# Moving a head's scores within SBUF: one DMA of 120 rows instead of two of 60

## The chip, the cores and the metric

The program runs on one core of a Trainium2 chip. The metric is the device time of one execution in microseconds. The kernel before takes 1316.79 us in the median of three runs (1316.54 to 1318.35).

## The reference

Talking-heads attention, then two feed-forward stages, all in float32 (batch 4, 12 heads, 448 positions, head size 64):

```python
scores = scale * np.matmul(q, k.transpose(0, 1, 3, 2))
scores = np.einsum('bhij,hg->bgij', scores, w_pre)        # mixes the heads
scores = scores - np.max(scores, axis=-1, keepdims=True)
attn = np.exp(scores)
attn = attn / (np.sum(attn, axis=-1, keepdims=True) + 1e-09)
attn = np.einsum('bhij,hg->bgij', attn, w_post)           # mixes the heads again
x = np.matmul(attn, v)                                    # rows of 12 * 64 = 768
h = ((x @ w1) * (x @ w2)) @ w3 @ w_out
h = h @ w_in2
out = np.maximum(0.01 * h, h) @ w_out2
```

## The kernel before

Attention comes first, the feed-forward stages (called MoE in the code) follow. Everything in attention is issued in an order written out by hand (`manual_schedule`, line 114): on each engine and each DMA queue the instructions stand in program order. The feed-forward part is ordered by a planner, with a few edges to attention's instructions (`issue_after`).

**Tiles.** The 448 query positions of a batch are cut into chunks of 120, 120, 120 and 90 (`CH` is 120; the last chunk is padded from 88 to 90). There are 16 chunks. The heads go in six pairs. `qk(b, c, p)` (line 178) multiplies a pair: two products of 120 x 448 scores into PSUM, one for each head. `out` (line 191) evicts them to a tile `s` (two heads, six buffers); ScalarE does both, except in the first eight calls (`early`), where VectorE takes the second head.

**The move.** Mixing the heads needs the heads along the partitions. So each head's scores are moved within SBUF by DMA from `s`, where a partition is a query position, to a tile `sr`, where 12 partitions of each of 10 groups are the heads of one query position (`move`, line 207). A DMA carries 60 rows of 448 floats, six to each of 10 destination partitions. A chunk of 120 has two such halves in two `sr` tiles; five tiles are used in turn (`SUB = 6`, lines 126 and 183). The last head needs two DMAs for a half, since its partitions wrap. So a chunk costs 26 DMAs, all issued by SyncE's queue (SP). The host has laid out the query columns (`_deal`, line 936) so that rows land in the right places.

**The mix and what follows.** `premix(k)` (line 240) is the first mix, for a group of 20 query positions: it reads two rows of the tile `sr`. A chunk has six groups, the last chunk of a batch five; there are 92 groups. The loop at line 406 handles two groups in one pass, `k` and `k + 1`. In the order of the code a pass does: stores of finished outputs (`flush`); `qk` for the pairs that groups `k + 8` and `k + 9` bring (`LEAD` is 8); row maxima on VectorE (`tops`); exponentials on ScalarE (`softmax`); the evictions and moves of this pass's pairs (`evict`); products with the values (`av`, line 314); division by the sums (`weigh`); the second mix of the pass before and its transposes (`postmix`); loads of later queries, keys and values (`side`); the first mix of groups `k + 2` and `k + 3`.

A chunk's first group needs all six pairs. The groups of a batch are 23, an odd count. In batches 0 and 2 a chunk starts on an even group, and its last pair is evicted one pass before its first `premix`. In batches 1 and 3 a chunk starts on an odd group, and its last pair is evicted and moved in the very pass whose end holds its first `premix`. The exception is the last chunk of a batch, whose last two pairs come a pass earlier.

**The start.** Before the loop the first eight groups' pairs (chunk 0 and two pairs of chunk 1) are multiplied, evicted and moved, and `premix(0)` and `premix(1)` follow. The `sr` tiles are zeroed first (`constants_load`, line 132).

**The end of attention.** The feed-forward part loads the attention output of two batches into `x` (line 648) behind entries of the list `reads`, which holds the moves in the order of issue: `XREADS = (-5, -3)`. The splitting of `x` on ScalarE and VectorE (`halves`) is placed behind the ends of certain passes (`XMARKS`). After the loop, lines 440 to 448 finish the remaining `av` products.

Of the kernel before, what the change touches and what calls it, by code (L numbers as in the profile page):

```python
# [8 lines left out]
F32 = mybir.dt.float32  # L9
# [13 lines left out]
def attention_moe_kernel(ctx: ExitStack, tc, qt, kt, vt, w_pre, w_post, w1, w2, w3t, w_out, w_in2, w_out2, out):  # L23
# [7 lines left out]
    nc = tc.nc  # L31
    B, _, NPAIR, S = kt.shape
# [6 lines left out]
    P = 128  # L39
    JP = 112  # L40
    NJ = S // JP
    IB = 10
    LEAD, SUB, GAP = 8, 6, 13
    CH = qt.shape[-1]
    scale = 1.0 / float(D) ** 0.5

# [3 lines left out]
    i0 = 0  # L50
# [17 lines left out]
    def bank(shape, name):  # L68
        return ps.tile(shape, F32, tag="bank", name=name, bufs=8)
# [34 lines left out]
    ends, reads, marks = {}, [], []  # L104

    def attention():
        with ExitStack() as es:
            ld = es.enter_context(tc.tile_pool(name="a_ld", bufs=2))
            big = es.enter_context(tc.tile_pool(name="a_big", bufs=1))
            const = es.enter_context(tc.tile_pool(name="a_const", bufs=1))  # L110
# [5 lines left out]
            HR, Q = HQ * H, P // 2  # L116
# [5 lines left out]
            kpre = const.tile([P, Q], F32, name="kpre")  # L122
            kpost = const.tile([P, 2, 32], F32, name="kpost")
            mask = const.tile([P, 2, HQ], F32, name="mask")
            eye = const.tile([P, HQ * GAP], F32, name="eye")
            rows_of = [const.tile([P, SUB, S], F32, name=f"sr{i}") for i in range(5)]
            wrep = const.tile([P, 2, H], F32, name="wrep")

            ones = const.tile([P, P], F32, name="ones")
# [1 line left out]

            def constants_load():
                for i, t in enumerate(rows_of):
                    (nc.gpsimd if i > 1 else nc.vector).memset(t, 0.0)
                for t in (kpre, kpost, eye):
                    nc.gpsimd.memset(t, 0.0)
                for n, w in enumerate((w_pre, w_post)):
                    nc.sync.dma_start(out=wrep[:, n, :], in_=w)
# [22 lines left out]
            vst, srt = {}, {}  # L161
            pms, mxs, ets, apt = {}, {}, {}, {}
# [15 lines left out]
            def qk(b, c, p, early=False):  # L178

                m = cols[c]  # L180
                if p == 0:
                    for i, n0 in enumerate(range(0, m, SUB * IB)):
                        srt[b, c, i] = rows_of[len(srt) % len(rows_of)], n0, min(SUB, (m - n0) // IB)
                t = big.tile([CH, 2, S], F32, tag="s", name="s", bufs=6)
                pq = [bank([CH, S], "pq") for _ in range(2)]
                for e in range(2):
                    rows = slice(e * D, (e + 1) * D)
                    nc.tensor.matmul(  # L188
                        pq[e][:m], qls[b, c][rows, p, :m], kls[b, p // 2][rows, p % 2, :], start=True, stop=True
                    )  # L190
                def out():
                    for e in range(2):
                        if e and early:
                            nc.vector.tensor_copy(t[:m, e, :], pq[e][:m])
                        else:
                            nc.scalar.activation(out=t[:m, e, :], in_=pq[e][:m], func=ACTF.Copy)  # L196
                    for e in range(2):
                        h = 2 * p + e
                        for i in range(2):
                            if (b, c, i) in srt:  # L200
                                move(srt[b, c, i], t[:, e, :], h)

                evs.append(out)
                if early:
                    evict()

            def move(sr, t, h):

                dst, n0, w = sr
                if h < H - 1:  # L210
                    parts = [(h, 0, 2 * HQ)]
                else:
                    parts = [(h, 0, HQ), (Q, HQ, HQ)]
                for r0, i0, n in parts:
                    reads.append(nc.sync.dma_start(  # L215
                        out=dst[r0:r0 + GAP * (n - 1) + 1:GAP, :w, :],
                        in_=t[n0 + i0 * w:n0 + (i0 + n) * w, :],
                    ))
                ends["sync"] = reads[-1]

            evs = []

# [17 lines left out]
            def premix(k):  # L240

                b, c, t, _ = where[k]
                i, u = divmod(t, SUB // 2)
                sr = srt[b, c, i][0]
                ns = groups[k]
                for n in ns:
                    pms[n] = bank([P, S], "pm")
                for s in range(2):
                    rows = slice(s * Q, (s + 1) * Q)
                    for g in range(len(ns)):  # L250
                        half = (g if len(ns) > 1 else s) * Q
                        nc.tensor.matmul(  # L252
                            pms[ns[s % len(ns)]][half:half + Q], kpre[rows], sr[rows, 2 * u + g, :],
                            start=True, stop=True,
                        )

# [17 lines left out]
            def weigh(ns, sm, e, last):  # L274

                m = len(ns)
                nc.vector.tensor_scalar(out=sm[:, :m], in0=sm[:, :m], scalar1=1e-9, scalar2=None, op0=ALU.add)
                rc = wk.tile([P, 2 * HB], F32, tag="rc", name="rc", bufs=2)
                ends["dve"] = nc.vector.reciprocal(out=rc[:, :m], in_=sm[:, :m])  # L279
                shares = (nc.gpsimd, nc.scalar, nc.vector, nc.scalar) if last else (nc.gpsimd,) * 3 + (nc.vector,)  # L280
                for i, eng in enumerate(shares[:m]):
                    if eng is nc.scalar:
                        ends["act"] = eng.activation(out=e[:, i], in_=e[:, i], func=ACTF.Copy, scale=rc[:, i:i + 1])
                        continue
                    ends["dve" if eng is nc.vector else "pool"] = eng.tensor_scalar(  # L285
                        out=e[:, i], in0=e[:, i], scalar1=rc[:, i:i + 1], scalar2=None, op0=ALU.mult
                    )
# [61 lines left out]
            for b, c in order:  # L349
                ns = [n for n, x in enumerate(blocks) if x[:2] == (b, c)]  # L350
# [54 lines left out]
            todo = []  # L405
            for k in range(0, NG + 2, 2):
                if k:
                    flush()
                while later:
                    stores.append(later.pop(0))  # L410
                now = [g for g in (k, k + 1) if g < NG]
                done = [g for g in (k - 2, k - 1) if g >= 0]
                fresh = [n for g in now for n in groups[g]]
                old = [n for g in done for n in groups[g]]
                before = ets.pop(k - 2, None)
                ahead = [x for g in now if g + LEAD < NG for x in slot(g + LEAD)]
                for x in ahead:
                    qk(*x)
                if fresh:
                    tops(fresh)  # L420
                    sm, ets[k] = softmax(fresh)
                evict()
                if now:
                    for _ in range(min(4 if len(todo) > NPAIR else 2, len(todo))):
                        av(*todo.pop(0))
                    weigh(fresh, sm, ets[k], not ahead)
                while lows:
                    lows.pop(0)()
                if old:
                    postmix(old, before)  # L430
                side(k // 2)
                for g in done:
                    b, c, t, nt = where[g]
                    if t == nt - 1 and (b, c) != order[-1]:
                        todo += [(b, c, p) for p in range(NPAIR)]
                for g in (k + 2, k + 3):
                    if g < NG:
                        premix(g)
                marks.append(dict(ends))
            while todo:  # L440
                av(*todo.pop(0))
            flush()
            for p in range(NPAIR):
                av(*order[-1], p)
# [491 lines left out]
def _deal(q, width=120):  # L936

    import numpy as _np

    n, h, s, d = q.shape  # L940
    places = []
    for c0 in range(0, s, width):
        at = [c0] * width
        for o in range(0, min(width, s - c0 + 2), 60):
            w = min(6, (s - c0 + 2 - o) // 10)
            for i in range(10):
                for m in range(w):
                    half, k = divmod(i, 5)
                    if m == w - 1 and w % 2:
                        to = 20 * (m // 2) + 5 * half + k  # L950
                    else:
                        to = 20 * (m // 2) + 10 * half + 5 * (m % 2) + k
                    at[o + i * w + m] = min(c0 + o + to, s - 1)
        places.append(at)
    places = _np.array(places)
    t = q[:, :, places, :].reshape(n, h // 2, 2, *places.shape, d)
    return t.transpose(0, 3, 2, 5, 1, 4).reshape(n, len(places), 2 * d, h // 2, width)
# [39 lines left out]
```

## Time and profile before

| | |
|---|---|
| median of 3 runs | 1316.79 us |
| the profiled execution | 1318.09 us |
| its span | 1316.3 us |
| TensorE matmul busy | 1240.1 us (94%) |
| VectorE busy | 892.1 us (68%) |
| ScalarE busy | 523.1 us (40%) |
| mean granted TensorE clock | 0.966 |
| DMAs of `sr<-s` | 416, of which 308 of 105 KB, 100 of 52.5 KB, 8 of 26.2 KB |

The span is what the profiler recorded from the first to the last instruction; the execution is 1.8 us longer. Engine names in rows: PE is TensorE's matmul, DVE VectorE, ACT ScalarE, POOL GpSimd, SPq SyncE's queue. In the rows `sr<-s` is the move, L252 the first mix, L188 `qk`, L329 `av`, L305 the second mix, L196 and L194 the evictions. The granted clock is a share of full speed: 1.00 is 2.4 GHz, 0.50 is 1.2 GHz.

### The profile page before, as it was taken

To read this page: it belongs to the slowest core of one execution; us is meant where nothing else is said; L and a number is where in the kernel's file an instruction comes from. 1 tells how busy PE (TensorE), PEld (TensorE's weight loads), DVE (VectorE), ACT (ScalarE), POOL (GpSimd) and SP (SyncE) were. 2 spreads that over 40 slices of the span, in tenths; PEclk is the share of its full clock that TensorE was granted. 3 is DMA by queue.
4 is the path that set the end of the run, shared out by engine and by line. 5 is a ranking of instruction groups with operands and counts; after the bars stand their busy time and mean duration, and the time that the engine had idled before them with its cause. 6 is when DMAs were issued, how large, how long until landed. Compare 5 with 4: busy or idle time off the path is not lost.

```text
span 1316.3 us, 22208 instructions
## 1 busy us (share of the span) xinstructions
PE 1240.1 (94%) x8616; PEld 981.9 (75%) x8616; DVE 892.1 (68%) x1552; ACT 523.1 (40%) x1024; POOL 195.6 (15%) x142
## 2 busy tenths in 40 slices
PE   5888989987897899999999999999999999999998
PEld 3233434443343589999889999999999999999998
DVE  3665657666566899983579596856877657394763
ACT  2645455544444455542235452335232333431220
POOL 2544445445442000000000000000000000000000
PEclk7888889999898899999999999999999999999999
DMA  4554544654533577563985463605342212212112
GB/s 153 171 158 139 167 136 127 176 161 139 167 110 127 185 243 235 178 205 136 357 308 191 169 208 127 218 25 204 107 126 84 80 55 73 72 43 67 30 49 84
DMA packets 124969, 190.51 MB, mean 145 GB/s; under 512 B 21600, under 2 KB 104640, under 8 KB 124480
## 3 DMA queue, kind: packets, MB, share of 16 engines
q1 hardware_dynamic: 124864, 189.10, 45.0%
q8 instruction: 68, 1.11, 0.4%
q14 instruction: 37, 0.30, 0.1%
HBM read 111.03 MB, written 39.32 MB: 114 GB/s over the span
## 4 chain that ended last, share of the span: by engine, by line
PE 80%; DMA 6%; DVE 5%; ACT 4%; SPq 3%; issue 1%; POOLq 0%; ACTq 0%; DVEq 0%
PE pm L480 27%; PE po L495 18%; PE pp L770 16%; PE pw L561 5%; DMA sr<-s 5%; PE pq L188 5%; PE pm L252 4%; SPq L215 3%; PE px L329 3%; DVE ap L312 3%; PE po L305 3%; ACT e L269 2%; ACT s L196 2%; DMA scr<-y 1%; DVE mx L262 1%
## 5 line engine op out<-in xcount | busy, mean ns | idle before, releaser
L480 PE MATMUL pm<-x,ws 128*128 128x384 f32 (+1 forms) x1152 | 233.9, 364 | 0.6 <-DVE ws L75 0.6
L480 PEld LDWEIGHTS pm<-x,ws 128*128 128x128 f32 x1152 | 208.7, 188 | 24.8 <-DVE ws L75 1.0
L285 POOL TENSOR_SCALAR e<-e,rc 128x448 f32<-128x448 f32 x130 | 187.9, 1458 | 244.0 <-DVE rc L279 204.2
L269 ACT ACTIVATE e<-pm,mx 128x448 f32<-128x448 f32 x180 | 111.9, 632 | 201.9 <-DVE mx L262 201.7
L252 PE MATMUL pm<-sr,kpre 64*64 64x448 f32 x720 | 104.2, 619 | 56.8 <-DMA sr<-s 52.6
L262 DVE TENSOR_REDUCE mx<-pm 128x1 f32<-128x448 f32 x180 | 100.3, 606 | 52.5 <-PE pm L252 52.3
L252 PEld LDWEIGHTS pm<-sr,kpre 64*64 64x64 f32 x720 | 30.9, 144 | 126.3 <-issue 87.1
L770 PE MATMUL pp<-t,w 128*128 128x448 f32 x576 | 124.5, 368 | 0.0
L312 DVE STREAM_TRANSPOSE ap<-po 128x512 f32<-128x512 f32 (+3 forms) x216 | 115.1, 592 | 13.1 <-PE po L305 12.0
L495 PE MATMUL po<-ws,g 128*128 128x384 f32 x672 | 117.2, 334 | 0.0
L495 PE MATMUL po<-wo,g 128*128 128x384 f32 x672 | 117.1, 334 | 0.0
L495 PEld LDWEIGHTS po<-wo,g 128*128 128x128 f32 x672 | 116.6, 188 | 0.2
L495 PEld LDWEIGHTS po<-ws,g 128*128 128x128 f32 x672 | 116.6, 188 | 0.0
L770 PEld LDWEIGHTS pp<-t,w 128*128 128x128 f32 x576 | 108.1, 188 | 10.9
L329 PEld LDWEIGHTS px<-ap,vs 96*64 96x64 f32 (+1 forms) x1536 | 80.4, 140 | 36.0 <-ACT e L269 21.0
L305 PE MATMUL po<-e,kpost 64*32 64x512 f32 (+1 forms) x1472 | 92.9, 598 | 11.9 <-ACT e L269 6.2
L188 PE MATMUL pq<-kl,ql 64*120 64x448 f32 (+1 forms) x384 | 97.5, 619 | 0.0
L770 PE MATMUL pp<-b,w 128*128 128x448 f32 x432 | 95.6, 368 | 0.0
L196 ACT ACTIVATE s<-pq 120x448 f32<-120x448 f32 (+1 forms) x184 | 86.0, 559 | 15.8 <-PE pq L188 13.4
L329 PE MATMUL px<-ap,vs 96*64 96x120 f32 (+3 forms) x1536 | 90.1, 271 | 2.0 <-DVE ap L312 1.2
L502 DVE TENSOR_TENSOR acc<-po,acc 128x384 f32<-128x384 f32 x84 | 45.3, 553 | 68.3 <-PE po L495 68.2
L91 ACT ACTIVATE wc<-wr 128x768 f32<-128x768 f32 (+1 forms) x72 | 61.6, 858 | 72.3 <-DMA wr<-in_moe_w_dram 21.6
(102 smaller groups left out, 1521.3 us busy)
## 6 DMA issues: line engine op xcount, KB each, us to landing
sr<-s SPq DMA_DIRECT2D x308, 105.0 KB
wr<-in_moe_w_out_dram SPq DMA_DIRECT2D x24, 768.0 KB
wr<-in_moe_w_dram SPq DMA_DIRECT2D x16, 768.0 KB
wr<-in_moe_w_in_dram SPq DMA_DIRECT2D x16, 768.0 KB
wr<-in_moe_w_dram SPq DMA_DIRECT2D x16, 512.0 KB
kept_w<-wc SPq DMA_DIRECT2D x16, 384.0 KB
sa<-kept_w SPq DMA_DIRECT2D x16, 384.0 KB
sums_w<-su SPq DMA_DIRECT2D x8, 768.0 KB
```

The costliest lines, as they stand in the source:

```text
L188: nc.tensor.matmul(pq[e][:m], qls[b, c][rows, p, :m], kls[b, p // 2][rows, p % 2, :], start=True, stop=True)
L196: nc.scalar.activation(out=t[:m, e, :], in_=pq[e][:m], func=ACTF.Copy)
L252: nc.tensor.matmul(pms[ns[s % len(ns)]][half:half + Q], kpre[rows], sr[rows, 2 * u + g, :], start=True, stop=True,)
L262: nc.vector.tensor_reduce(out=mxs[n], in_=pms[n], axis=AX.X, op=ALU.max, negate=True)
L269: ends["act"] = nc.scalar.activation(out=e[:, i], in_=pms.pop(n), func=ACTF.Exp, bias=mxs.pop(n), scale=1.0, accum_out=sm[:, i:i + 1])
L285: ends["dve" if eng is nc.vector else "pool"] = eng.tensor_scalar(out=e[:, i], in0=e[:, i], scalar1=rc[:, i:i + 1], scalar2=None, op0=ALU.mult
L305: nc.tensor.matmul(po[g][32 * r:32 * (r + 1), :m], kpost[rows, x], e[rows, :m, JS[r]:JS[r] + P], start=True, stop=True,)
L312: ends["dve"] = nc.vector.transpose(out=dst, in_=po[g][:, i0:i1])
L329: nc.tensor.matmul(px[e * D:(e + 1) * D, r, :nw].rearrange("p (n i) -> p n i", i=HQ), vst[b][rows, jc, 2 * p + e, :], ap[rows, x, :ns, jc, ...
L480: nc.tensor.matmul(dst, wt[:, a, kk, :], x[kk][:, c, c0:c0 + w], start=(kk == order[0] and j == 0), stop=(kk == order[-1] and j == 2),)
L495: nc.tensor.matmul(po, g[m][:, a, t * P:(t + 1) * P], wts[m][:, c, cs], start=(m == 0 and j == 0), stop=(m == FQ - 1 and j == 2),)
L770: nc.tensor.matmul(dst, w[:, i, a, kk, :], b[:, kk, c, :], start=(kk == 0 and j == 0), stop=(kk == KH - 1 and j == 2),)
```

## The change

A head's scores of a whole chunk go in one DMA: 120 rows, 12 to each of 10 destination partitions; the last head in two DMAs of 60 rows. A chunk has one `sr` tile of 12 rows, and three such tiles are used in turn. The tile `s` has five buffers instead of six. In the first eight calls (`early`) ScalarE's queue issues the move of the first head of a pair; everything else stays on SP. The remaining `av` products of the pass that has no new groups are placed ahead of its second mix instead of after the loop. `_deal` lays out the queries for whole chunks. `XREADS` is not edited; the list it counts in has half as many entries.

```diff
-    LEAD, SUB, GAP = 8, 6, 13
+    LEAD, GAP = 8, 13
...
-            rows_of = [const.tile([P, SUB, S], F32, name=f"sr{i}") for i in range(5)]
+            rows_of = [const.tile([P, CH // IB, S], F32, name=f"sr{i}") for i in range(3)]
...
-                    (nc.gpsimd if i > 1 else nc.vector).memset(t, 0.0)
+                    (nc.gpsimd if i else nc.vector).memset(t, 0.0)
...
                 if p == 0:
-                    for i, n0 in enumerate(range(0, m, SUB * IB)):
-                        srt[b, c, i] = rows_of[len(srt) % len(rows_of)], n0, min(SUB, (m - n0) // IB)
-                t = big.tile([CH, 2, S], F32, tag="s", name="s", bufs=6)
+                    srt[b, c] = rows_of[len(srt) % len(rows_of)]
+                t = big.tile([CH, 2, S], F32, tag="s", name="s", bufs=5)
...
                     for e in range(2):
-                        h = 2 * p + e
-                        for i in range(2):
-                            if (b, c, i) in srt:
-                                move(srt[b, c, i], t[:, e, :], h)
+                        move(srt[b, c], t[:m, e, :], 2 * p + e, nc.sync if e or not early else nc.scalar)
...
-            def move(sr, t, h):
-
-                dst, n0, w = sr
+            def move(dst, t, h, queue):
+
+                m = t.shape[0]
+                w = m // IB
...
                 for r0, i0, n in parts:
-                    reads.append(nc.sync.dma_start(
-                        out=dst[r0:r0 + GAP * (n - 1) + 1:GAP, :w, :],
-                        in_=t[n0 + i0 * w:n0 + (i0 + n) * w, :],
-                    ))
-                ends["sync"] = reads[-1]
+                    ends["sync"] = queue.dma_start(
+                        out=dst[r0:r0 + GAP * (n - 1) + 1:GAP, :w, :], in_=t[i0 * w:(i0 + n) * w, :]
+                    )
+                    reads.append(ends["sync"])
...
-                i, u = divmod(t, SUB // 2)
-                sr = srt[b, c, i][0]
+                sr = srt[b, c]
...
-                            pms[ns[s % len(ns)]][half:half + Q], kpre[rows], sr[rows, 2 * u + g, :],
+                            pms[ns[s % len(ns)]][half:half + Q], kpre[rows], sr[rows, 2 * t + g, :],
...
                     weigh(fresh, sm, ets[k], not ahead)
+                else:
+                    while todo:
+                        av(*todo.pop(0))
                 while lows:
                     lows.pop(0)()
...
-            while todo:
-                av(*todo.pop(0))
             flush()
```

## Rows read from the trace of the kernel before

**Rows 1.** Busy time of each engine in stretches; then granted clock, DMA share, GB/s.
```profile
14.00:26.00 12.00, 0.14 (x2) 0.00 (x0) 1.53 (x5) 0.54 (x1) 0.00 (x0) 0.69 0.43 130
52.00:60.00 8.00, 8.00 (x66) 2.63 (x62) 5.34 (x10) 4.65 (x12) 3.02 (x3) 0.75 0.94 239
100.00:150.00 50.00, 42.63 (x506) 19.74 (x502) 31.55 (x72) 24.29 (x67) 24.67 (x18) 0.90 0.56 160
125.00:131.00 6.00, 6.00 (x23) 2.14 (x21) 1.59 (x4) 2.90 (x8) 1.79 (x2) 0.50 0.54 140
500.00:550.00 50.00, 50.00 (x250) 44.95 (x249) 48.30 (x75) 24.78 (x37) 0.00 (x0) 1.00 0.63 202
```

**Rows 2.** Who waited for whom in attention: us in total, times, longest.
```profile
PE pm L252 <- DMA sr<-s: 52.6, 12, 14.4
```

**Rows 3.** Timeline of SP's queue: start, duration, operation, count.
```profile
7.52 28.24 SPq L215 DMA_DIRECT2D sr<-s  x34
...
396.69 11.30 SPq L215 DMA_DIRECT2D sr<-s  x14
```

**Rows 4.** Source line 215: ns min/median/max of one issue, first and last start.
```profile
L215 SPq DMA_DIRECT2D sr<-s x416: 712/748/2812, 7.5 to 407.3; - x139
```

**Rows 5.** Timeline at the start of attention, ScalarE and TensorE.
```profile
9.66 0.54 ACT L196 ACTIVATE s<-pq 120x448 f32<-120x448 f32 x1 [2.16 <-PE pq L188]
...
28.52 3.78 PE L252 MATMUL pm<-sr,kpre 64*64 64x448 f32 x16 [14.38 <-DMA sr<-s]
```

**Rows 6.** The chain that ended last, in pieces: start, duration, what.
```profile
42.15 2.54 DMA sr<-s
...
48.39 2.29 DMA sr<-s
...
131.13 7.59 DMA sr<-s
...
146.05 1.73 ACT s L196 x4
...
407.26 1.99 DMA sr<-s
```

**Rows 7.** Timeline of TensorE, first mixes of chunks in batches 0 and 2.
```profile
50.78 4.12 PE L252 MATMUL pm<-sr,kpre 64*64 64x448 f32 x16 [3.96 <-DMA sr<-s]
...
77.47 4.03 PE L252 MATMUL pm<-sr,kpre 64*64 64x448 f32 x16 [4.22 <-DMA sr<-s]
...
229.19 2.11 PE L252 MATMUL pm<-sr,kpre 64*64 64x448 f32 x16 [1.59 <-DMA sr<-s]
...
281.70 3.42 PE L252 MATMUL pm<-sr,kpre 64*64 64x448 f32 x16 [4.04 <-DMA sr<-s]
...
307.32 2.07 PE L252 MATMUL pm<-sr,kpre 64*64 64x448 f32 x16 [1.12 <-DMA sr<-s]
```

**Rows 8.** Timeline of TensorE around first mixes of chunks in batches 1 and 3.
```profile
141.11 1.74 PE L252 MATMUL pm<-sr,kpre 64*64 64x448 f32 x16
142.78 1.77 PE L188 MATMUL pq<-kl,ql 64*120 64x448 f32 x8
...
147.80 0.98 PE L252 MATMUL pm<-sr,kpre 64*64 64x448 f32 x8
151.59 2.48 PE L252 MATMUL pm<-sr,kpre 64*64 64x448 f32 x8 [2.81 <-DMA sr<-s]
154.01 3.35 PE L188 MATMUL pq<-kl,ql 64*120 64x448 f32 x8
...
382.51 2.14 PE L252 MATMUL pm<-sr,kpre 64*64 64x448 f32 x8 [1.65 <-issue]
```

**Rows 9.** End of attention: TensorE's timeline, and a piece of the chain.
```profile
407.45 1.68 PE L252 MATMUL pm<-sr,kpre 64*64 64x448 f32 x8 [1.31 <-DMA sr<-s]
...
409.38 6.35 DMA x<-scr
...
440.27 2.82 PE L305 MATMUL po<-e,kpost 64*32 64x384 f32 x32 [4.23 <-POOL e L285]
```

More of the change, by code (lines that the diff above doesn't have):

```diff
@@ L943, in _deal @@
         at = [c0] * width
[L944 to L953, printed above, removed]
+        w = min(width, s - c0 + 2) // 10
+        for i in range(10):
+            for m in range(w):
+                half, k = divmod(i, 5)
+                to = 5 * half if m == w - 1 and w % 2 else 10 * half + 5 * (m % 2)
+                at[i * w + m] = min(c0 + 20 * (m // 2) + to + k, s - 1)
         places.append(at)
```

## The prediction

> **What bounds the kernel now.** I read first the busy time by stretches. TensorE is busy for all of a stretch of the feed-forward part, at the full clock; in attention it is busy 42.6 us of 50, at a mean clock of 0.90 [rows 1]. So the second part has nothing to give, and it starts when attention's last results are there: a microsecond saved in attention is a microsecond of the whole. The list of waits says what TensorE lacks in attention: its first mix waited 52.6 us for moves, in 12 places, the longest 14.4 us [rows 2]. Then SP's timeline: the first 34 moves occupy the queue without a break for 28.24 us, that is 0.83 us each, and the last 14 for 11.30 us, 0.81 us each [rows 3]. An issue takes 712 ns at least and 748 ns in the median over moves of 15 to 60 rows [rows 4]; its cost goes by the count of DMAs, not by their rows. A pass with two new pairs issues 8 to 10 of them, 6.5 to 8.3 us, and a pass of TensorE at full clock, from one `premix` to the next, takes 147.80 - 141.11 = 6.7 us [rows 8]. SP is the engine that can't keep up. Last I read TensorE's own timeline where a chunk begins: it stops there [rows 7, 8], and what runs after a long stop runs slowly. The stretch from 125 to 131 us, behind such a stop, shows the granted clock at 0.50, the 1.2 GHz level [rows 1].
>
> **Part 1: the start.** `premix(0)` begins at 28.52 us after 14.38 us of idling [rows 5]. It waits for the 23rd issue of SP, at 0.83 us each, and its landing. After the change it needs 13 moves, 7 on SP and 6 on ScalarE. ScalarE's cycle for a pair is one eviction (0.54 us [rows 5]) and one issue (0.8 us, taken as on SP [rows 4]), some 1.4 us, so five pairs after 9.66 us end by 16.9 us; SP is done earlier. Then the transfers limit. The highest rate in my rows is 239 GB/s, at a DMA share of 0.94 [rows 1]; a move of 215 KB needs 0.90 us at it. The first move of the second pair goes out at about 9.66 + 0.54 + 0.05 = 10.25 us. It lands 3.2 us later (below), nine more heads follow at 0.90 us: 10.25 + 3.2 + 8.1 = 21.5 us. The gain is 28.5 - 21.5 = **7.0 us**. Bounds: 9.5 us if issue alone limits (last issue 16.1 us, landing 19); nothing or a loss of 2 us if ScalarE's issues cost twice as much and its evictions wait behind them. The five `s` buffers make the sixth pair wait for the first pair's landing, about 11.6 us, before its turn. The three larger memsets stay ahead: they write the same order of bytes as before, and the DMA of the first chunk waits only for VectorE's one.
>
> At this place a page weighs against me. The startup rows show a DMA share of 0.43 at 130 GB/s [rows 1], so the engines had room. The Trainium skill, "DMA: Bandwidth & Descriptors", section "Why a DMA increments its semaphore by 16 and not by 1", says that a DMA runs on the largest number of engines, up to 16, that divides the slowest dimension of both sides. For 120 source rows and 10 destination partitions that is ten, as for 60 rows. Then the share can't pass 10/16, the rate not 130 x 0.625 / 0.43 = 189 GB/s, a move takes 1.14 us and the start gains about 4.8 us instead of 7.0; no row here shows the engines one by one.
>
> **How long a move of 120 rows takes.** No row shows one. From issue to landing 15 rows took 1.99 us, 30 rows 2.29 us and 60 rows 2.54 us [rows 6]. Bounds: 2.54 us if rows cost nothing, 5.1 us if all of it doubles. The line through the first and last gives (2.54 - 1.99) / 45 = 12 ns a row, so 2.54 + 0.73 = 3.2 us; I take this, and 2.8 us for the last head's 60 rows on five partitions. The issue I leave at 0.8 us.
>
> **Part 2: chunks in batches 0 and 2.** After its `qk` a pass evicts from +3.2 to +5.0 us (146.05 to 147.78 against 142.78 [rows 6, 8]). With a free queue its five moves go out from +3.8 us, the last at +7.0, landing by +10.2. The `premix` that needs them is in the next pass, 5.0 + 6.7 = +11.7 us. So the wait goes, with 1.5 us to spare. The five waits add up to 3.96 + 4.22 + 1.59 + 4.04 + 1.12 = 14.9 us, and the mixes behind them took 4.12, 4.03, 2.11, 3.42 and 2.07 us where one at full clock takes 1.74 [rows 7, 8], 7.1 us more. Gain **22.0 us**.
>
> **Part 3: chunks in batches 1 and 3.** Six chunks have their last pair's move in the pass that needs it. Their waits are what is left of the 52.6 us: 52.6 - 14.4 - 14.9 - 1.3 (the one in the tail) = 22.0, with the sixth, 1.65 us, which the view files under "issue" [rows 2, 8, 9]: 23.6 us. Behind them the mix took 2.48 for 0.98 us and `qk` 3.35 for 1.77 us [rows 8]; five times 3.1 and once 2.4 us make 18. Together 41.6 us. Here moving faster doesn't remove the wait. Take the one at 151.59: TensorE was ready at 148.78; the first head's eviction ends at about 146.5, its move goes out then, the last head's two at 147.3 and 148.1, and they land at 150.1 and 150.9. The first products need only the first. The wait is 1.3 us and 0.3 us more inside the mix: 1.6 us instead of 2.8. What of it lowers the clock is unsure: of the three waits of 1.65, 1.59 and 1.12 us, the first was followed by a slow mix (2.14 for 0.98), the others lost 0.3 us [rows 7, 8]; I put 1.0 us on each. Left: 6 x 2.6 = 15.6 us; gain **26.0 us**. If landing took 5.1 us, each would cost 2 us more.
>
> **Part 4: the end.** The load of `x` goes out at 409.38 us, when the last move has landed (407.26 + 1.99 [rows 6]), and takes 6.35 us [rows 9]; ScalarE, VectorE and so TensorE stand behind it in order. Half as many moves in the last pass with moves: seven from 396.7 us, the last issued at 401.5, landed at 404.4. The load moves up by **4.8 us** and the tail with it. The wait of 1.3 us at the last chunk lies inside this and isn't counted again. `XREADS` now names earlier heads, but the load still stands behind landings of `s`; if it were put between the last moves it would hold SP about 2.5 us. The `av` products put ahead of the last mix (two, about as long as that mix at full clock, 1.9 us) fall into the 4.23 us in which TensorE waits for GpSimd there [rows 9]. Behind it VectorE's and ScalarE's conversions for the next part run anyway, so I count a third of it; bounds 0 and 1.9. Gain **0.7 us**.
>
> **Part 5: edits at nothing.** Five `s` buffers: a pair's eviction waits for the landing two and a half passes earlier, some 17 us; the longest landing shown, behind a load of the values, is 7.59 us [rows 6]. That is the cover; without it ScalarE would stand before its evictions. The addressing in `premix` changes no instruction.
>
> **Sum.** 7.0 + 22.0 + 26.0 + 4.8 + 0.7 = 60.5 us, and 1 us for small waits that I didn't list: 61.5. The profiled execution took 1318.1 us; 1256.6. The median of the runs is 1.3 us lower: **1255 us**.
>
> **Rivals.**
> - *Transfers take the queue's place.* SP's time goes, but the longer moves land at 4 to 5 us, the start gains 3, the six waits of part 3 stay at 2.8 us and keep their slow mixes (gain 41.6 - 6 x 5.9 = 6), the first five still go (22), the tail gives 4 or so: 35 us, 1282 us. For it: the DMA share stood at 0.94 when a load and moves met [rows 1]. Against: 0.5 otherwise.
> - *The remaining waits vanish as well*, because evictions run earlier once TensorE isn't slow: 15.6 us more, 1240 us. For it: little; the wait is a chain inside one pass.
> - *The issue goes by rows after all, and it is slower.* A move of 120 rows holds its queue 1.6 us. Then SP is as late as now, and each chunk's first mix waits for the whole chunk instead of its first half: two issues, 1.6 us, and 0.7 us of landing, at 14 starts, 32 us; the start gains 4, the result is 1317 + 28 = 1345 us. It decides from about 1.4 us an issue. Against it: 712 to 748 ns from 15 to 60 rows [rows 4].
> - *It does nothing*: another engine holds the passes at their present length. Against: passes of 6.7 us with no wait stand between the stops [rows 8].
>
> **Chances.** Forecast 0.64 (its own range 1243 to 1268), transfers 0.22, all waits gone 0.07, slower 0.05, nothing 0.02. The range of 8 in 10 is 1239 to 1284. Faster by over 0.2% (about what a measurement of this kernel can tell from no change) 0.93, within 0.02, slower 0.05.
>
> **What will show it.** Right: SP's first moves end by 17 us, `premix(0)` starts between 19 and 24 us; an issue stays under 0.9 us; no wait at chunks of batches 0 and 2, and waits of 1 to 2.5 us at six chunks of 1 and 3; `x` is loaded 4 to 5 us sooner after the last `qk`; the feed-forward part keeps its length. Wrong: an issue above 1.2 us, landings above 4.5 us, waits of ScalarE on landings of `s` within the loop, or a clock of 0.50 in long stretches without a stop before them.

## The result, and the profile after

The changed kernel takes 1296.16 us in the median of 4 runs (1293.3 to 1298.52) and the kernel before 1316.66 us on the same chip: a ratio of 0.9845 [0.9819, 0.987]. It is faster, by 20.5 us where 61 were forecast, and lies outside the range. The profiled execution took 1296.13 us, its span 1294.3 us.

Three points of the trace divide the 22.0 us between the two spans:

| us | last first mix ends | first product of the feed-forward part | end |
|---|---|---|---|
| before | 431.0 | 451.5 | 1316.3 |
| after | 400.95 | 426.9 | 1294.35 |

The rows of the last first mix and, before, of the first product (L480); the one after (L476) stands further below. The second row shows the last six products of that mix:

```profile
429.08 1.94 PE L252 MATMUL pm<-sr,kpre 64*64 64x448 f32 x12
...
451.47 0.73 PE L480 MATMUL pm<-x,ws 128*128 128x512 f32 x2
```

```profile
399.66 1.29 PE L247 MATMUL pm<-sr,kpre 64*64 64x448 f32 x6
```

Attention's mixes end 30.1 us sooner. The stretch from there to the feed-forward part grows from 20.4 to 26.0 us, and that part itself from 864.8 to 867.4: 30.1 - 5.5 - 2.6 = 22.0. So two questions are open: why attention gave 30 us and not 55, and what took 8 us back at the join, that is, between attention's last first mix and the feed-forward part.

The first can be split by batch. The last first mix of each of the four batches ends at 118.59, 222.15, 322.85 and 431.02 us before, and at 110.98, 208.87, 296.04 and 400.95 us after. So the start gave 4.9 us, batches 0 and 2 gave 16.2 (2.7 and 13.5), and batches 1 and 3 gave 8.9 (5.7 and 3.2, with the tail up to the last first mix); 7.0, 22.0 and 26.0 were forecast. Two thirds of what is missing lie in batches 1 and 3.

Of the page after, the chain of work that ended last, by engine (names in `q` are queues, `issue` is time in which the engine waited for nothing that the profile shows), and the group of the first mixes (busy and mean ns; idle time and what ended it, in answer to [rows 2]):

```profile
PE 82%; DMA 6%; DVE 6%; ACT 4%; issue 1%; SPq 0%; ACTq 0%; DVEq 0%
...
L247 PE MATMUL pm<-sr,kpre 64*64 64x448 f32 x720 | 100.4, 594 | 32.2 <-DMA sr<-s 20.7
```

SP's queue has left the chain (3% before); moves are still in it. The source line of the move, in answer to [rows 4], and SP's timeline at the start, in answer to [rows 3]:

```profile
L212 SPq DMA_DIRECT2D sr<-s x200: 721/756/1733, 8.4 to 375.1; - x100
L212 ACTq DMA_DIRECT2D sr<-s x8: 785/854/1453, 8.3 to 20.8; - x8
```

```profile
8.38 15.72 SPq L212 DMA_DIRECT2D sr<-s  x9
24.15 1.49 SPq L176 DMA_DIRECT2D ql<-in_q_dram  x1
31.67 10.19 SPq L212 DMA_DIRECT2D sr<-s  x9
```

An issue takes 756 ns in the median over SP's 200 moves of 45 to 120 rows, 124 of them of 120, where 15 to 60 rows took 748: it goes by the DMA. Nine issues at the start stretch over 15.72 us, however. Part of that is waiting: for VectorE's evictions, and for 4.6 us, in four places, for landings of earlier moves. The last head's second DMA goes out at 18.57 us, when a move that ScalarE issued at 12.37 has landed, and lands 7.43 us later, at 26.00. TensorE's start and a chunk that begins in batch 1, in answer to [rows 5, 8]:

```profile
23.58 1.76 PE L247 MATMUL pm<-sr,kpre 64*64 64x448 f32 x4 [8.72 <-DMA sr<-s]
26.04 3.25 PE L247 MATMUL pm<-sr,kpre 64*64 64x448 f32 x12 [0.70 <-DMA sr<-s]
...
104.56 1.77 PE L187 MATMUL pq<-kl,ql 64*120 64x448 f32 x8
...
110.01 0.97 PE L247 MATMUL pm<-sr,kpre 64*64 64x448 f32 x4
113.28 0.97 PE L247 MATMUL pm<-sr,kpre 64*64 64x448 f32 x4 [2.30 <-ACT e L264]
114.97 1.24 PE L247 MATMUL pm<-sr,kpre 64*64 64x448 f32 x4 [0.73 <-DMA sr<-s]
```

The row at 113.28 names ScalarE's exponential, which had ended at 107.8: the wait is one for the last head's first DMA, issued at 109.24 and landed at 113.08. The chain that ended last, there, has the second one:

```profile
107.91 1.75 ACT s L195 x4
109.65 0.35 SPq L212
110.00 0.05 issue
110.05 4.79 DMA sr<-s
114.84 0.14 issue
114.97 1.24 PE pm L247 x4
```

It took 4.79 us to land. The stretches of [rows 1] again: granted clock, DMA share and GB/s are the last three columns, and the third is new, at the join.

```profile
14.00:26.00 12.00, 2.62 (x10) 0.46 (x6) 2.96 (x11) 2.18 (x4) 0.00 (x0) 0.75 0.62 193
100.00:150.00 50.00, 44.23 (x493) 19.16 (x493) 29.73 (x68) 24.35 (x66) 25.91 (x18) 0.90 0.55 156
...
422.00:433.00 11.00, 5.86 (x13) 4.31 (x14) 9.77 (x15) 5.06 (x6) 0.00 (x0) 0.53 0.76 233
```

Last the join, in answer to [rows 9]: SP's timeline, and TensorE's.

```profile
401.11 13.30 SPq L228 DMA_DIRECT2D scr<-y  x2
414.45 1.53 SPq L83 DMA_DIRECT2D wr<-in_moe_w_dram  x2
```

```profile
414.83 5.67 PE L324 MATMUL px<-ap,vs 96*64 96x90 f32 x96 [2.97 <-DVE ap L307]
426.94 1.86 PE L476 MATMUL pm<-x,ws 128*128 128x512 f32 x4 [6.44 <-ACT ws L72]
```

Two stores of outputs span 13.30 us of the queue, since the second waits for a tile that VectorE copies at 413.2. The feed-forward part's first weights (`wr`) stand behind it. TensorE waits 6.44 us for what ScalarE and VectorE make of them (`ws`), and from 422 to 433 us the clock is 0.53 in the mean.

### The profile page after: what moved, and what is told of

Read it like the earlier page. It is cut to its first block, busy times and chain, and to the rows that moved or that the text cites. A ratio compares the mean times of both kernels' runs of the same rounds, so it can differ in the third digit from the quotient of the medians.

```text
span 1294.3 us, 21888 instructions
## 1 busy us (share of the span) xinstructions
PE 1238.5 (96%) x8616; PEld 981.2 (76%) x8616; DVE 889.0 (69%) x1551; ACT 524.0 (40%) x1024; POOL 198.5 (15%) x141
## 3 DMA queue, kind: packets, MB, share of 16 engines
q8 instruction: 68, 1.11, 0.4%
## 4 chain that ended last, share of the span: by engine, by line
PE 82%; DMA 6%; DVE 6%; ACT 4%; issue 1%; SPq 0%; ACTq 0%; DVEq 0%
PE pm L476 27%; PE po L491 18%; PE pp L766 16%; PE pw L557 5%; DMA sr<-s 5%; PE pq L187 4%; PE pm L247 4%; PE px L324 4%; DVE ap L307 3%; ACT e L264 3%; PE po L300 3%; ACT s L195 1%; DVE mx L257 1%; DMA wr<-in_moe_w_dram 1%; PE turn L234 1%
## 5 line engine op out<-in xcount | busy, mean ns | idle before, releaser
L476 PE MATMUL pm<-x,ws 128*128 128x512 f32 (+1 forms) x1152 | 236.5, 366 | 6.6 <-ACT ws L72 6.4
L476 PEld LDWEIGHTS pm<-x,ws 128*128 128x128 f32 x1152 | 210.6, 189 | 31.7 <-ACT ws L72 6.6
L247 PE MATMUL pm<-sr,kpre 64*64 64x448 f32 x720 | 100.4, 594 | 32.2 <-DMA sr<-s 20.7
L247 PEld LDWEIGHTS pm<-sr,kpre 64*64 64x64 f32 x720 | 27.8, 140 | 103.5 <-issue 49.8
```

Of the source, the lines that this page charges most:

```text
L247: nc.tensor.matmul(pms[ns[s % len(ns)]][half:half + Q], kpre[rows], sr[rows, 2 * t + g, :], start=True, stop=True,)
L476: nc.tensor.matmul(dst, wt[:, a, kk, :], x[kk][:, c, c0:c0 + w], start=(kk == order[0] and j == 0), stop=(kk == order[-1] and j == 2),)
```

## The experiments

My theory after this: (1) the `av` edit moved the weight loads behind a store; (2) the last head's two DMAs, on five destination partitions each, are slow, and they set the six waits of batches 1 and 3; (3) each of these waits is a chain inside one pass, so that shorter transfers shrink it but only more lead removes it. The rivals: the order of the tail is worth nothing; transfers are slow at any shape; ScalarE's issuing is what helps or hurts.

**The `av` edit undone.**

```diff
-                else:
-                    while todo:
-                        av(*todo.pop(0))
...
+            while todo:
+                av(*todo.pop(0))
             flush()
```

> The changed kernel with one edit undone: the remaining av products stand behind the loop again. Theory A: the edit cost time. It brought the last but one store of attention ahead of the first weight loads in SP's queue; the store waits for VectorE, and the loads go out 13.5 us after the last first-mix where before they went out 0.8 us after it. Undone, the loads go out within 2 us of it, the first feed-forward product starts 5 to 8 us earlier, and the time is 1287 to 1291 us. Theory B: the loads are late because the larger sr tile or the shifted layout holds their memory. Then nothing moves: 1295 to 1297 us.

Measured: 1288.77 us, 0.9791 [0.9769, 0.9814], 7.4 us under the changed kernel. SP's timeline, and TensorE's (lines move up by one):

```profile
401.21 0.57 SPq L228 DMA_DIRECT2D scr<-y  x1
401.82 1.53 SPq L83 DMA_DIRECT2D wr<-in_moe_w_dram  x2
...
417.28 0.57 SPq L228 DMA_DIRECT2D scr<-y  x1
```

```profile
421.83 1.08 PE L475 MATMUL pm<-x,ws 128*128 128x512 f32 x4 [1.15 <-ACT ws L72]
```

Weights are loaded 12.6 us sooner, ahead of the late store, and the wait of 6.44 us is 1.15. The edit cost time. The trace shows where 5.2 us of it went: the join takes 20.8 us instead of 26.0. In the execution traced the feed-forward part was 1.4 us longer, and this execution lies 3.6 us above the median; what makes up the rest of the 7.4 is not shown.

**SP issues every move.** `nc.sync` in place of `nc.sync if e or not early else nc.scalar`.

> The changed kernel with every move on SP's queue, the first ones too. Theory A: at the start the transfers limit (ten engines, about 1.2 us a move), not the issue; premix(0) starts within 1 us of 23.6 us and the time is within 2 us of 1296. Theory B: ScalarE's half of the issues gave the 5 us that the start gained; premix(0) starts at 26 us or later and the time is 1298 to 1301 us.

Measured: 1291.4 us, 0.9806 [0.9782, 0.9829], 4.8 us under the changed kernel. `premix(0)` starts at 24.35 us instead of 23.58, but runs without a break and ends at 28.55, where in the changed kernel it waits for the last head's second DMA and ends at 29.29: the second queue is worth nothing there. What I had not expected is the rest: `premix(2)` starts at 30.57 us against 32.50 in the changed kernel, and one at 75.77 against 80.13. Of the two waits that the changed kernel has there, the first is still there with SP alone (1.09 us, at 44.1), the second is gone:

```profile
46.36 0.97 PE L247 MATMUL pm<-sr,kpre 64*64 64x448 f32 x4 [1.41 <-ACT s L195]
...
70.71 4.07 PE L247 MATMUL pm<-sr,kpre 64*64 64x448 f32 x16 [3.28 <-DMA sr<-s]
```

**The last head on nine partitions and one.**

```diff
-                    parts = [(h, 0, HQ), (Q, HQ, HQ)]
+                    parts = [(h, 0, 2 * HQ - 1), (Q + GAP * (HQ - 1), 2 * HQ - 1, 1)]
```

(and `mask` over all thirteen partitions of a group).

> The changed kernel with the last head's rows split 108 + 12 instead of 60 + 60: nine destination partitions in one DMA, one partition in the other (the unused thirteenth place of a group takes the rows; the result is that of the reference). Same bytes, same count of DMAs. Theory A: a DMA of five destination partitions runs on five engines, and both halves on the same five, so the two take 1.5 to 1.8 us each; with nine and twelve engines the last head lands 1.5 to 2.5 us earlier. The six waits of batches 1 and 3, now 2.5 to 3.4 us, become 1 to 1.8 us: 8 to 14 us less, 1282 to 1288 us. Theory B: landing goes by rows and by the queue, not by the number of partitions: within 2 us of 1296.

Measured: 1268.97 us, 0.9635 [0.9611, 0.9659], 27 us under the changed kernel and more than I had put on it. Of the moves only the shape of 16 pairs of DMAs was changed. Of the 27.2 us between the two traces' last first mixes, 18.6 lie in batches 1 and 3 and 8.0 in batch 0, for which the expectation had nothing. TensorE where the same chunk begins:

```profile
97.04 1.77 PE L187 MATMUL pq<-kl,ql 64*120 64x448 f32 x8
...
105.39 1.09 PE L247 MATMUL pm<-sr,kpre 64*64 64x448 f32 x8 [1.94 <-issue]
```

The last head's two DMAs, issued at 101.72 and 102.54, land 3.48 and 2.84 us later (3.84 and 4.79 before the edit). The wait is 1.94 us and the mix is whole behind it, at full clock; the other five are 2.12 to 2.64 us. In the first 520 us the trace has the clock at 0.50 for 41 us; 72 in the changed kernel, 89 before.

**Every head on five partitions and five.** `parts = [(h, 0, HQ), (h + GAP * HQ, HQ, HQ)]`: 24 DMAs a chunk for 13, with the same bytes.

> The changed kernel with every 120-row move cut in two DMAs of 60 rows by destination: five partitions each, 12 rows on each. Bytes as before; 24 DMAs a chunk where the kernel before had 26. Theory A: a DMA runs on as many engines as it has destination partitions, the lowest ones, so all moves share five engines: eight DMAs of some 1.5 us a pass are 12 us where a pass takes 7; the moves set the pace, attention takes 150 to 220 us longer, 1440 to 1520 us. Theory B: issue count is what matters: as the kernel before, 1310 to 1325 us.

Measured, in a single run: 1364.69 us, 68 over the changed kernel. The direction is theory A's, its size is not (1440 or more was forecast). Waits of TensorE for moves (us, times, longest), and a stretch at the start in which nothing but such DMAs goes out, from two queues:

```profile
PE pm L247 <- DMA sr<-s: 87.9, 15, 14.4
```

```profile
20.00:33.00 13.00, 0.00 (x0) 0.00 (x0) 1.16 (x2) 2.18 (x4) 0.00 (x0) 0.50 0.33 119
```

The DMA share stops at 0.33 and 119 GB/s, while every DMA takes about 7 us to land; the changed kernel's start, mostly moves to ten partitions, had 0.62 and 193 GB/s. 5/16 is 0.31 and 10/16 is 0.625. A head of 215 KB costs 1.8 us at the one rate and 1.1 at the other. This is also why the forecast of 1440 us was too long: at 119 GB/s a DMA of 60 rows takes 0.9 us and not 1.5, so eight of them about fill a pass of 6.7 us and do not take 12.

**Two repairs together**, `av` back and nine and one; **and SP alone** beside them.

> The kernel after with two edits together: the remaining av products back behind the loop, and the last head's DMA split over nine destination partitions and one. Theory A (the two costs lie in different places, the tail and the loop): they add up. 1269.0 (nine and one alone) less 7.4 (av back alone, against after) = 1261.5 us; first weight load within 1 us of the last first mix, the first feed-forward product about 21 us after it instead of 26. Theory B (both end in the same slow stretch at the join, so that one of them hides the other): 1266 to 1270.

> As the run before it, and every move issued by SP. Theory A (ScalarE's issues delay its evictions at the start, whatever the split): another 4 to 6 us, 1256 to 1258. Theory B (the loss came from the last head's two DMAs on five partitions landing behind the moves of two queues, and with nine and one it is gone): 1260 to 1263, the same within 0.2%, and premix(0) at 24.1 to 24.5 us in both.

Measured: 1267.58 us, 0.9641 [0.9614, 0.9668], and 1264.78 us, 0.9616 [0.9588, 0.9643]. Neither is told from 1268.97 by its interval; the first lies in its theory B's range, the second above both of its own. In the trace the join does what theory A says (20.7 us from the last mix to the first product, 26.3 with the `av` edit), yet attention was 1.3 us longer in that execution; the runs of these three kernels scatter by 8 to 10 us. These two do not decide whether the gains add up.

**Ten groups of lead**, on top of these three edits.

```diff
-    LEAD, GAP = 8, 13
+    LEAD, GAP = 10, 13
...
-            for k in range(LEAD):
+            for k in range(8):
...
             premix(1)
+            for k in range(8, LEAD):
+                for x in slot(k):
+                    qk(*x, early=True)
```

> As the run before it, and from the first pass of the loop on the pairs come ten groups ahead instead of eight, so that the last pair of a chunk in batches 1 and 3 is evicted and moved one pass before the pass that needs it. Theory A (the six waits that are left are a chain inside one pass: qk, eviction, move, landing): they go, 6 x (2.2 us and 0.5 to 1 us of slow clock behind it), 16 to 19 us, 1238 to 1243; waits for moves in the loop under 3 us in sum. Theory B (the DMA engines are behind by then, whatever the time of issue): waits over 1 us stay at four or more of the six chunks, 1250 to 1257.

Measured: 1241.43 us, 0.9432 [0.9414, 0.945], 23.3 us under the same kernel with a lead of eight; the fastest here. TensorE's waits for moves, and a stretch of it:

```profile
PE pm L247 <- DMA sr<-s: 8.7, 1, 8.7
```

```profile
100.00:150.00 50.00, 49.69 (x621) 23.12 (x618) 40.02 (x94) 30.49 (x85) 31.14 (x22) 1.00 0.67 200
```

The one wait left is that of `premix(0)`. TensorE is busy 49.69 us of 50 at full clock, with a higher DMA share than before: transfers had room, the moves were late.

**The same lead with five and five**, and **that with ScalarE issuing** as in the changed kernel.

> The run with ten groups of lead, and the last head's DMA on five and five partitions as in the kernel after. Theory A (with a whole pass in hand a landing of 4 to 5 us is covered; only at the start, and where a load lies beside the moves, do the five engines still cost): 1243 to 1250 us, waits for moves in the loop under 4 us in sum. Theory B (the doubled time of the last head on five engines delays all that stands behind it in the DMA engines, at any lead): 1258 to 1270, waits over 1 us at four or more chunks.

> The run with ten groups of lead and five and five partitions, with ScalarE's queue issuing the first heads' moves of the early pairs, as in the kernel after. Theory A (ScalarE's issues cost time by themselves: its exponentials and evictions of the first passes come later): 1247 to 1251, 4 to 6 us slower than with SP alone. Theory B (what they cost in the kernel after was the lateness of moves that a pass was waiting for): within 0.2%, 1241 to 1246.

Measured: 1243.31 us, 0.9437 [0.9421, 0.9452], and 1244.02 us, 0.9448 [0.9429, 0.9467]. With a pass more of lead the shape that was worth 27 us makes a difference of 1.9 us, which the intervals do not tell from none (one wait is left in the loop, 1.22 us at 71.0), and the second queue's loss is gone. Both had cost time only where a pass was waiting for a move.

**The kernel before, with one edit each**: nine and one; and ten groups of lead, first with its five tiles, then with a sixth tile and five buffers of `s`.

> The kernel before, with the last head's DMAs of 60 rows split over nine destination partitions and one instead of five and five. Theory A (before, SP's queue is the bound; the count of its DMAs is unchanged, so a quicker last transfer saves its landing alone): 12 waits shorter by 0.3 to 0.5 us and some slow mixes, 1308 to 1315. Theory B (before, too, it is the transfers on five partitions that hold TensorE at a chunk's start): most of the 22 to 27 us that the same edit gave the kernel after, 1288 to 1298.

> The kernel before, with pairs ten groups ahead from the first pass of the loop on. Theory A (SP's issues are the bound before: 26 moves of 0.8 us are 20.8 us for a chunk, a chunk's three passes 20.1 us, and loads and stores come on top): the lead turns into a backlog on SP and helps at part of the chunks, 1290 to 1306. Theory B (only the lead was short, and one DMA for 120 rows was never needed): near 1250 to 1262, with waits for moves under 6 us after the start.

> The kernel before, ten groups of lead, with a sixth tile of moved rows (so that no move writes rows that a later mix still reads) and five buffers of s. Theory A (SP's issues are the bound before: a chunk's 26 moves and its loads take over 20.8 us, its three passes 20.1): the lead hides part of the waits until SP has fallen behind again, 1285 to 1306. Theory B (the lead was all that was missing): 1245 to 1262, waits for moves under 6 us after the start.

Measured: 1315.42 us, 0.9997 [0.9984, 1.0009] for the split: nothing, less than even theory A. For the lead with five tiles 1337.28 us, 1.0149 [1.0125, 1.0172]: there a tile is given to a chunk whose moves overwrite rows that a mix still ahead reads, so this mix gets the later chunk's rows and waits for their moves (16.97 us at 105.6); it says nothing on the bound. With six tiles 1302.63 us, 0.9892 [0.9869, 0.9915], inside theory A's range. Its waits for moves, and SP's timeline:

```profile
PE pm L252 <- DMA sr<-s: 31.4, 8, 14.4
```

```profile
94.59 18.03 SPq L215 DMA_DIRECT2D sr<-s  x22
112.72 0.62 SPq L232 DMA_DIRECT2D scr<-y  x1
113.43 6.92 SPq L215 DMA_DIRECT2D sr<-s  x8
```

The queue issues without a pause, 0.82 to 0.87 us each, and TensorE waits 5.43 us at 125.4. The lead is worth 14 us on the kernel before and 44.8 on the changed one (1288.77 to 1244.02, two kernels with the `av` edit undone that differ in the lead alone). So SP's issues did bound the kernel before, as the prediction read it; the change took that bound away, and another one stood right behind it.

## Why the prediction was wrong, point by point

- **What bounds the kernel now:** right. SP left the chain, and one edit without the other (a split or a lead on the kernel before) gives 0 and 14 us.
- **The issue:** right, 0.756 us for 0.8. The first head's move of a pass, alone in the queues, lands 3.24 us after its issue (108.37 to 111.61), for 3.2.
- **The start:** 4.9 us for 7.0. The forecast took 0.90 us a move from a stretch in which loads and moves ran at 239 GB/s; the moves alone went at 193 GB/s, 1.11 us each. The Trainium skill, "DMA: Bandwidth & Descriptors", section "Why a DMA increments its semaphore by 16 and not by 1", gave ten engines; the estimate worked out from it, 189 GB/s, 1.14 us and a gain of 4.8 us, was weighed and left. The share of 0.62 agrees with it. The gain is smaller still at the mix's end, 29.29 us for 32.30, since its last products wait for the last head's second DMA.
- **Batches 0 and 2:** of the five waits, 14.9 us, three are gone. Two are left, both in batch 0: 1.41 us at 46.4 with 0.59 more inside the mix, and 3.28 us at 70.7. Both are waits for the last head's DMAs again, which took 6.0 and 6.7 us to land before the first and 9.2 and 9.4 before the second, with loads issued beside them; the forecast had them land in 3.2. With nine partitions and one the first wait is gone and the second is 1.87 us.
- **Batches 1 and 3: the step that failed.** The chain was right up to the landing: after a `qk` at 104.56 the last head's DMAs go out 4.7 and 5.5 us later (forecast 4.5 and 5.3). The term was "2.8 us for the last head's 60 rows on five partitions". They took 3.84 and 4.79 us. So the wait was 2.30 and 0.73 us where 1.3 and 0.3 were forecast, and the six, with what is left inside their mixes, add up to 17.5 us instead of 9.6. The second term that was too small hangs on it, "I put 1.0 us on each" for the slow clock behind a wait: five of the six are followed by 6.8 us at a clock of 0.50 and one by 3.4. TensorE is busy for 35.4 us of that, which at half the clock is some 17.7 us lost where 6 were left in the sum, and the same 35.4 us were spent so behind the six waits before: the change took nothing off it. The two terms are 8 and 12 us short.

  For the landing, I had priced a move by its rows along a line through [rows 6], where the largest transfer puts six rows on a partition; both DMAs of the last head put twelve, on half as many partitions as the other heads.

  The same section of the Trainium skill says that such a DMA runs on five engines, and always on the lowest-numbered ones, so that these two queue behind each other and behind every other move. That agrees with the share of 0.33 where two queues issue nothing else. No row names the engines, but their number can be counted in the trace, in the increments of the semaphore that tells of a landing (no view prints them): a load from DRAM has 16, a move to ten partitions 11, each DMA of the last head 6, and after the split into nine and one 10 and 13. One of those of a move stands apart, some 1.2 us after the issue; the others are ten, five, nine and twelve, the numbers that the rule gives. With nine partitions and one the term is 2.84 to 3.48 us, the wait 1.94 us, three of the six waits are followed by no slow clock, and the median is 1268.97, which the range would have held.
- **The end:** `x` is loaded 12.8 us after the last `qk` begins and 16.5 us before, 3.7 us sooner for 4.8. The `av` edit was entered as a gain of 0.7 us, bounds 0 and 1.9. It cost 7.4 us here (with nine and one in place, undoing it gave 1.4, within the noise), because I looked at the products on TensorE and not at what the edit does to SP: VectorE's copy and its store come with the products, and the weight loads stand behind that store.
- **Edits at nothing:** no eviction waits for a landing in the loop, and two do at the start, 2.9 and 1.1 us. No run has the change with six buffers.
- **The feed-forward part keeps its length:** not quite, 2.6 us longer, of which most is the slow clock at the join. With `av` back it is still 1 to 4 us longer than before (866.0 to 868.8 against 864.8); this stays open.
- **The rivals:** "transfers take the queue's place" was the right mechanism, at 1282 us, with the six waits at 2.8 us and their slow mixes kept. Landings above 4.5 us, one of the prediction's signs of being wrong, came too. The `av` edit and the two waits at the start of the loop carried the result beyond it.

## What to carry to other kernels

Price a DMA within SBUF by the partitions it reaches as well as by its rows, and look at the one with the odd shape: it lands last, and the consumer waits for it. Book the slow clock behind a wait in full unless the wait itself goes. When a bound is taken away, lay out the rest of the chain from producer to consumer; if it does not fit between them, faster links only shorten the wait, and starting one pass earlier removes it. For an instruction moved at the end of a stage, list the stores that come with it, and the next stage's loads behind them in that queue.

## What the runs showed of the hardware that I had not expected

- The DMA share stood at 0.62 with moves to ten partitions and at 0.33 with moves to five, both from two queues. With moves to ten and SP alone it was 0.60 (14 to 26 us): a second queue does not raise it.
- A second issuing queue brought the first product of `premix(0)` forward by 0.8 us and its end back by 0.7: from the fifth move of chunk 0 on a landing took 6.0 to 7.8 us, where SP alone had 4.2 to 5.5.
- In the changed kernel the six waits of batches 1 and 3 cost about twice their length: behind them the clock is at 0.50 for 3.4 or 6.8 us, in which a first mix of eight took 1.99 to 3.15 us instead of 0.98. The length of the wait alone does not tell: with nine and one a wait of 2.22 us has a slow stretch behind it and one of 2.25 us has none.
